# A channel product in seven products per pair of row tiles, and a reordered gate, in a three-part transformer kernel on one Trainium2 core

## The chip, the cores and the metric

The kernel runs on one core of a Trainium2 chip. The core has a matrix engine (TensorE, PE), which multiplies a stationary weight tile of 128 x 128 by a moving tile of up to 512 columns and adds into banks of PSUM; three engines for elementwise work (VectorE or DVE, ScalarE or ACT, GpSimd or POOL); and SyncE (SP), which here issues all DMA transfers. The engines run side by side, each in the order of its own instructions, and wait for each other through semaphores. The metric is the time of one execution in device microseconds. The time before is 1161.88 us, the median of 3 runs (1161.79 to 1162.14).

## The reference

Three parts on 8 batches of 576 tokens and 512 channels, each on the output of the one before: chunked attention, a mixer, a gated layer.

```
# 1 attention: 8 heads of 64, chunks of 64 tokens
scores = scale * q_c @ k_c.T;  attn = exp(scores - max) / (sum + 1e-9);  x = attn @ v_c
# 2 mixer: token product, then channel product
h  = relu(x.T @ w_tok1) @ w_tok2          # 576 -> 256 -> 576, over tokens
u  = x + h.T
h2 = relu(u @ w_ch1) @ w_ch2              # 512 -> 1536 -> 512, over channels
x  = u + h2
# 3 gated layer
h  = relu(x @ w_in);  u, v = split(h)     # 512 -> 1024, halves of 512
v_n = (v - mean(v)) / sqrt(var(v) + 1e-6)
v_s = w_spatial @ v_n + b_spatial         # 576 x 576, over tokens
out = (u * v_s) @ w_out                   # 512 -> 512
```

## The kernel before

All products are done in fp16 with both operands split: a high part (the value rounded to fp16) and a low part (the value less its high part). Each product is three products, high x high, high x low, low x high, added in PSUM in fp32. A split costs one copy for the high part, mostly on ACT, and one subtraction for the low part on DVE or POOL.

Per batch PE does, in this order: the first channel product (`ch1`, 12 row tiles m of 24 matmuls of 288 columns, inner dimension 4 x 128, weights `c1w` resident in SBUF); the second (`ch2`, four tiles of 72 matmuls of 288); two of the pending output projections of the batch before (`proj`, 12 matmuls of 512 columns each); the gate's v half (`gate_v`, five token tiles); the first token product of the *next* batch (`tok1`, 28 matmuls of 512); four gated blocks (`gated`: a `gate_u` of 24 matmuls and a `spatial` of 28, the u block ahead of the spatial block for m = 0 and behind it for the others); the second token product of the next batch (`tok2`, four tiles of 12 matmuls of 288); the remaining projections. Attention of later batches is cut in steps (`a_step`), which a clock puts in between: `pump` adds an estimate for each matmul and calls the steps that are due (`pumps`, `attention_from`, which spreads a batch's attention over a span of 118000 units of this clock).

PE's order is the order of the code (`manual_schedule`). The order on DVE, ACT, POOL and SP is made by a scheduler, which follows dependencies and priority (`high_priority`). Two pools matter here. PSUM's pool `pm` has four tiles of two banks each, used in turn; the matmuls of a new tile wait until the tile's last reader is done. The working pool `wrk` has three buffers under the tag "t", used in turn by the temporaries of normalization, residual and gate.

Line numbers of the kernel before that the prediction uses: L435 is the matmul in `products`; L458 and L462 the two loops of `tok1`, L465 and L466 its evictions (relu to the high part on ACT, low part on DVE); L473 to L475 the update of x behind `tok2` and its split; L482 the low part of the residual on POOL; L558 the eviction of a v block; L600 and L611 the reads of PSUM of spatial and u; L613 and L614 the split of the gated product; L221 and L267 attention's matmuls; L212, L256 and L286 elementwise work of attention; L143 the split of weights, in the lead-in.

## Time and profile before

| | |
|---|---|
| median of 3 runs | 1161.88 us (1161.79 to 1162.14) |
| profiled execution | 1162.57 us, span 1160.8 us |
| mean granted clock of TensorE | 0.994 |
| PE busy | 1130.3 us (97%), 11256 matmuls |
| DVE, ACT, POOL busy | 572.9, 356.2, 190.2 us (49%, 31%, 16%) |

The span runs from the first to the last instruction. A line of a timeline gives the start, the time from there to the modelled end, the engine, the program's line, the operation and tiles, and a count; in brackets stands the idle time before it and what ended it. Matmuls overlap, so the price of one is read from the distance of two starts. The granted clock is given as a share of 2.4 GHz: 0.50 is the lower level, 1.2 GHz.

### The profile page before, as it was taken

Reading aid. Unit: us, or ns where it says so; the run is one execution under the profiler, and the core shown is the slowest. Engines: PE = TensorE matmul, PEld = TensorE weight load, DVE = VectorE, ACT = ScalarE, POOL = GpSimd, SP = SyncE. Lnnn points to the kernel's source line nnn. Section 1 sums busy time; section 2 is a strip of 40 time slices with the busy share of each in tenths; the row PEclk is TensorE's granted clock in tenths of the full one; section 3 lists DMA queues with packets and bytes.
Section 4 is the critical chain, followed back from the end, with each engine's and each line's share of the span. In section 5 each row is a group of like instructions: output and inputs, shape, how many; then the busy total and the mean of one; then the engine's idle time right before and its main releaser. Section 6 shows DMA issues by size and latency. Waiting matters only on the chain. (4 is left out here: it accounts for less than half of the span.)

```text
span 1160.8 us, 25354 instructions
## 1 busy us (share of the span) xinstructions
PE 1130.3 (97%) x11256; PEld 810.2 (70%) x11256; DVE 572.9 (49%) x1020; ACT 356.2 (31%) x568; POOL 190.2 (16%) x185
## 2 busy tenths in 40 slices
PE   5898989999999999999999999999999999999998
PEld 5576747776667766777576775777666775777765
DVE  6999987443643236533454424653363322441141
ACT  3334443332333223332224313242233222221121
POOL 0000032111310123102221022211131021200020
PEclk9899999999999999999999999999999999999999
DMA  9357613333222222223123220232211011000001
GB/s 318 119 200 234 208 34 73 70 68 79 38 68 49 42 60 38 60 46 56 46 38 88 62 49 25 49 88 43 60 34 37 19 27 30 1 1 1 19 19 46
DMA packets 92157, 76.68 MB, mean 66 GB/s; under 512 B 67600, under 2 KB 76816, under 8 KB 89744
## 3 DMA queue, kind: packets, MB, share of 16 engines
q1 hardware_dynamic: 92048, 75.06, 25.3%
q8 instruction: 88, 1.44, 0.5%
q14 instruction: 21, 0.17, 0.1%
HBM read 51.45 MB, written 9.44 MB: 52 GB/s over the span
## 5 line engine op out<-in xcount | busy, mean ns | idle before, releaser
L435 PE MATMUL mp<-xb,c1w 128*128 128x288 f16 x2304 | 288.3, 286 | 4.4 <-DVE xb L475 2.5
L522 PE MATMUL mp<-hb,c2w 128*128 128x288 f16 x2304 | 288.8, 286 | 3.0 <-DVE c2w L143 2.9
L435 PEld LDWEIGHTS <-c1w 128*128 128x128 f16 x2304 | 223.5, 98 | 63.7 <-DVE c1w L143 3.0
L522 PEld LDWEIGHTS <-c2w 128*128 128x128 f16 x2304 | 223.0, 98 | 60.9 <-DVE c2w L143 4.6
L513 DVE SCALAR_TENSOR_TENSOR hb<-mp,hb 128x576 f16<-128x576 f32 x96 | 72.5, 755 | 146.6 <-ACT hb L512 146.6
L435 PE MATMUL mp<-spw,vn 128*128 128x288 f16 x896 | 115.8, 286 | 0.0
L512 ACT ACTIVATE hb<-mp 128x576 f16<-128x576 f32 x96 | 62.3, 649 | 148.0 <-PE mp L435 147.9
L435 PEld LDWEIGHTS <-vn 128*128 128x128 f16 x896 | 86.7, 98 | 22.0
L435 PE MATMUL mp<-xb,inw 128*128 128x288 f16 x768 | 99.3, 286 | 0.0
L627 PE MATMUL mp<-otw,gb 128*128 128x512 f16 x432 | 96.0, 379 | 0.0
L435 PEld LDWEIGHTS <-inw 128*128 128x128 f16 x768 | 75.1, 98 | 20.4
L548 PE MATMUL mp<-inw,xb 128*128 128x512 f16 x384 | 84.7, 379 | 0.4 <-DVE xb L482 0.4
L480 DVE SCALAR_TENSOR_TENSOR rt<-mp,xT 128x576 f32<-128x576 f32 x32 | 24.1, 755 | 106.8 <-PE mp L522 106.8
L627 PEld LDWEIGHTS <-gb 128*128 128x128 f16 x432 | 42.1, 98 | 48.0
L482 POOL TENSOR_TENSOR xb<-rt,xb 128x576 f16<-128x576 f32 x22 | 30.4, 1384 | 275.1 <-ACT xb L481 275.1
L548 PEld LDWEIGHTS <-xb 128*128 128x128 f16 x384 | 37.3, 98 | 45.4 <-DVE xb L482 0.9
L286 POOL TENSOR_TENSOR xh<-xT,xh 128x512 f16<-128x512 f32 x24 | 27.8, 1158 | 247.4 <-ACT xh L283 226.4
L249 POOL TENSOR_TENSOR p<-sd,p 128x512 f16<-128x512 f32 (+1 forms) x30 | 34.7, 1156 | 159.9 <-ACT p L246 144.8
L481 ACT ACTIVATE xb<-rt 128x576 f16<-128x576 f32 x32 | 21.7, 681 | 126.3 <-DVE rt L480 126.3
L564 DVE BATCH_NORM_STATS2 st<-vt 128x6 f32<-128x512 f32 (+1 forms) x40 | 27.5, 690 | 58.2 <-ACT vt L558 57.9
L613 ACT ACTIVATE gb<-gt 128x576 f16<-128x576 f32 x32 | 21.8, 683 | 108.0 <-DVE gt L611 107.9
L435 PE MATMUL mp<-t2w,hb 128*128 128x288 f16 x384 | 50.3, 286 | 0.3 <-ACT hb L465 0.3
(144 smaller groups left out, 1137.8 us busy)
## 6 DMA issues: line engine op xcount, KB each, us to landing
qk<-in_qk SPq DMA_DIRECT2D x96, 128.0 KB, 2.8
out<-o SPq DMA_DIRECT2D x31, 256.0 KB, 2.0
v<-in_v SPq DMA_DIRECT2D x56, 128.0 KB, 3.3
vn<-in_wc SPq DMA_DIRECT2D x4, 1024.0 KB, 4.9
otw<-in_wc SPq DMA_DIRECT2D x3, 1024.0 KB, 4.8
spw<-in_wc SPq DMA_DIRECT2D x3, 1024.0 KB, 4.9
hb<-in_qk SPq DMA_DIRECT2D x4, 512.0 KB, 6.1
qk<-in_qk SPq DMA_DIRECT2D x4, 512.0 KB, 5.0
```

The costliest lines, as they stand in the source:

```text
L249: POOL.tensor_tensor(out=p_hl[rows, 1], in0=m["sd"][rows], in1=p_hl[rows, 0], op=ALU.subtract)
L286: POOL.tensor_tensor(out=m["lo"], in0=xT[:, :, tk], in1=m["hi"], op=ALU.subtract)
L435: PE.matmul(out=o, lhsT=l, rhs=r, start=(i == 0), stop=(i == len(seq) - 1))
L480: DVE.scalar_tensor_tensor(out=t, in0=ps, scalar=DN10, in1=two(x[:, m]), op0=ALU.mult, op1=ALU.add)
L482: eng.tensor_tensor(out=xl, in0=t, in1=xh, op=ALU.subtract)
L512: ACT.activation(out=hh, in_=ps, func=AF.Relu)
L513: DVE.scalar_tensor_tensor(out=hlo, in0=ps, scalar=0.0, in1=hh, op0=ALU.max, op1=ALU.subtract)
L522: PE.matmul(out=o, lhsT=c2w[:, a, k, mc], rhs=hb[:, k, r, s], start=(k + e == 0), stop=(k == 11 and e == 2))
L548: PE.matmul(out=ps, lhsT=l, rhs=r, start=(k + e == 0), stop=(k == 3 and e == len(seq) - 1))
L564: DVE.bn_stats(out=st[0:n], in_=t[0:n])
L613: ACT.activation(out=gh, in_=t, func=AF.Copy)
L627: PE.matmul(out=ps, lhsT=gb[:, l, k, tk], rhs=otw[:, r, k], start=(k == 0 and e == 0), stop=(k == 3 and e == 2))
```

## The change

For batches 2 to 7 `ch1` is replaced by `ch1_fast`. The 1536 output channels are six pairs p of row tiles; the product of a pair, inner dimension 512, and of the 576 columns is seen as a 2 x 2 block product: a11 to a22 are blocks of the weights (128 channels by 256), b11 to b22 blocks of x (256 channels by 288 tokens). It is done with seven products instead of eight, Winograd's form of Strassen's method, each of six matmuls of 288 columns. The sums of x (q1, q2, q3 and q1 again, `first_sums`) are made and split behind `tok2`; the sums of the weights (`sum_steps`, 30 steps in batch 1) are split and written to DRAM (`c1s`) and streamed back (`stream`), 128 KB for each product, in 18 slots in the place of `c1w`. Results are joined in PSUM, where two products can be added in place, and by DVE (`u2b`, `vb`, `c22`, `c`); the four blocks of hb are its output, whose layout changes, so that `ch2` reads it block by block.

The gate: u blocks are computed by `gate` between the v blocks (in batches 0 and 7 behind them) and kept in SBUF as `uall`; `gated` is then the spatial block and a multiplication of two tiles in SBUF. `tok2` moves in front of the spatial blocks, directly behind `tok1`. All four or five pending projections go behind `ch2`. The low parts of the gate go to POOL for all m except for the last one of the last batch, and the carry copies from DVE to ACT and POOL. The clock of attention's steps is scaled by `PACE` per stage, over a span of 112000.

Line numbers of the changed kernel that the prediction uses: L627 is the matmul in `product`; L504 the low part in `split`; L509 the update of x in `first_sums`; L515, L519, L521 and L523 the sums q1, q2, q3 and q1 again; L645 the sum `u2b`; L754 the read of the spatial block from PSUM; L766 the multiplication by `uall`; L769 the low part of the gated product; L450 the matmul in `products`, L477 the second loop of `tok1`. L241 to L254 and L225, L269 (DVE), L262 and L299 (POOL) are attention.

```diff
-    hb = new("hb", [128, 12, 2, S])
+    hb = new("hb", [128, 6, 2, 4, 288])
...
+    SLOTS = 18
+    ORDER = [(p, n) for p in range(7) for n in ((p, 0), (p, 4), (p - 1, 6), (p - 1, 2), (p, 3), (p, 5), (p, 1)) if 0 <= n[0] < 6]
+    ORDER = [n for _, n in ORDER]
+    uall = hall[:, 4608:9216].bitcast(F32).rearrange("p (m t) -> p m t", m=4)
+    tq4 = new("tq4", [128, 2, 2, 288])
+    quad = lambda t: t.rearrange("p (e k t) -> p e k t", e=2, k=2)
+    tq = [xb[:, :, 0:2, 288:576], quad(call[:, 9216:10368]), quad(call[:, 10368:11520]), tq4]
+    vals = vall.bitcast(F32)
+    s1b, u2b, vb, c22b = vals[:, 0:288], [vals[:, 288 + 288 * i:576 + 288 * i] for i in range(2)], vals[:, 864:1152], [
+        vals[:, 1152 + 288 * i:1440 + 288 * i] for i in range(2)]
+    c1s = tc.dram_tile([6, 128, 3584], F16, name="c1s")
...
-        clock[0] += cols / 2.4 + 2.5
+        t = cols / 2.4 + 2.5
+        clock[0] += t
+        slow[0] += t * pace[0]
         for p in pumps:
-            while p[3]() and clock[0] >= p[0]:
+            while p[3]() and p[4][0] >= p[0]:
...
+    PACE = {"first": 0.5, "pair": 0.8, "ch1": 1.0, "ch2": 1.2, "gate": 1.0, "tok1": 1.0, "last": 0.6}
+    sums = {}
+
+    def split(t, hi, lo, eng=DVE):
+        ACT.activation(out=hi, in_=t, func=AF.Copy)
+        eng.tensor_tensor(out=lo, in0=t, in1=hi, op=ALU.subtract)
+
+    def first_sums(ps, m, x):
+        t1, t2 = slice(0, 288), slice(288, 576)
+        xm = two(x[:, m])
+        DVE.scalar_tensor_tensor(out=xm, in0=ps, scalar=DN10, in1=xm, op0=ALU.mult, op1=ALU.add)
+        s = t1 if m < 2 else slice(0, 576)
+        split(x[:, m, s], xb[:, 0, m, s], xb[:, 1, m, s])
+        b11, b12, b21, b22 = x[:, 0:2, t1], x[:, 0:2, t2], x[:, 2:4, t1], x[:, 2:4, t2]
+        if m == 1:
+            sums[0] = t = wrk.tile([128, 2, 288], F32, tag="t", name="q1")
+            DVE.tensor_tensor(out=t, in0=b12, in1=b11, op=ALU.subtract)
+            split(t, tq[0][:, 0], tq[0][:, 1], POOL)
+        if m == 3:
+            q1, q2, q3 = sums[0], wrk.tile([128, 2, 288], F32, tag="t", name="q2"), wrk.tile([128, 2, 288], F32, tag="t", name="q3")
+            DVE.tensor_tensor(out=q2, in0=b22, in1=q1, op=ALU.subtract)
+            split(q2, tq[1][:, 0], tq[1][:, 1], POOL)
+            DVE.tensor_tensor(out=q3, in0=b22, in1=b12, op=ALU.subtract)
+            split(q3, tq[2][:, 0], tq[2][:, 1], POOL)
+            DVE.tensor_tensor(out=q1, in0=b21, in1=q2, op=ALU.subtract)
+            split(q1, tq[3][:, 0], tq[3][:, 1], POOL)
...
+            if fast:
+                return first_sums(ps, m, x)
...
-        hh, hlo = two(hb[:, m, 0]), two(hb[:, m, 1])
+        row = slice(m % 2 * 2, m % 2 * 2 + 2)
+        hh, hlo = hb[:, m // 2, 0, row], hb[:, m // 2, 1, row]
...
+    def stream(upto):
+        while streamed[0] < min(upto, 42 * (B - FIRST_FAST)):
+            p, n = ORDER[streamed[0] % 42]
+            SP.dma_start(out=call[:, streamed[0] % SLOTS * 512:streamed[0] % SLOTS * 512 + 512],
+                         in_=c1s[p, :, 512 * n:512 * n + 512])
+            streamed[0] += 1
+
+    used = [0]
...
+        def first():
+            POOL.tensor_tensor(out=s[:, 0], in0=a21, in1=a22, op=ALU.add)
+            POOL.tensor_tensor(out=s[:, 2], in0=a11, in1=a21, op=ALU.subtract)
+
+        def second():
+            POOL.tensor_tensor(out=s[:, 1], in0=s[:, 0], in1=a11, op=ALU.subtract)
+            POOL.tensor_tensor(out=s[:, 3], in0=a12, in1=s[:, 1], op=ALU.subtract)
+
+        def high():
+            ACT.activation(out=g[:, :, 0], in_=s, func=AF.Copy)
+
+        def low():
+            DVE.tensor_tensor(out=g[:, :, 1], in0=s, in1=g[:, :, 0], op=ALU.subtract)
+            SP.dma_start(out=c1s[p, :, 1536:3584], in_=vall[:, 0:2048])
+
+        return [join, first, second, high, low]
...
+        def product(o, p, n, b, start):
+            assert ORDER[used[0] % 42] == (p, n)
+            i = used[0] % SLOTS * 512
+            w = call[:, i:i + 512].rearrange("p (e k m) -> p e k m", e=2, k=2)
+            o = o[:, 0:288]
+            for k in range(2):
+                for i, (a, e) in enumerate(((0, 0), (0, 1), (1, 0))):
+                    PE.matmul(out=o, lhsT=w[:, a, k], rhs=b[:, e, k], start=(start and k + i == 0),
+                              stop=(k == 1 and i == 2), skip_group_check=not start)
+                    pump(288)
+            used[0] += 1
+            stream(used[0] + SLOTS)
+
+        def relu2(c, hi, lo):
+            ACT.activation(out=c, in_=c, func=AF.Relu)
+            split(c, hi, lo, POOL)
+
+        for p in range(7):
+            pace[0] = PACE["first" if p < 1 else "pair"]
+            if p < 6:
+                ab[p] = a = pm.tile([128, 2, 512], F32, tag="m", name="mp")
+                product(a[:, 0], p, 0, xb[:, :, 0:2, t1], True)
+                product(a[:, 1], p, 4, tq[1], True)
+                with high():
+                    ACT.activation(out=s1b, in_=a[:, 0, 0:288], func=AF.Copy)
+                    DVE.tensor_tensor(out=u2b[p % 2], in0=a[:, 1, 0:288], in1=s1b, op=ALU.add)
+            if p:
+                d, u = cd[p - 1], u2b[(p - 1) % 2]
+                product(d[:, 0], p - 1, 6, xb[:, :, 2:4, t2], False)
+                product(d[:, 1], p - 1, 2, tq[3], False)
+                c = wrk.tile([128, 2, 288], F32, tag="t", name="c")
+                with high():
+                    DVE.tensor_tensor(out=c, in0=d[:, :, 0:288], in1=u.rearrange("p (a t) -> p a t", a=1).to_broadcast([128, 2, 288]), op=ALU.add)
+                    relu2(c, hb[:, p - 1, 0, 1:3], hb[:, p - 1, 1, 1:3])
+            if p < 6:
+                cd[p] = d = pm.tile([128, 2, 512], F32, tag="m", name="mp")
+                c22 = c22b[p % 2]
+                product(d[:, 0], p, 3, tq[0], True)
+                product(d[:, 1], p, 5, tq[2], True)
+                with high():
+                    DVE.tensor_tensor(out=vb, in0=d[:, 0, 0:288], in1=u2b[p % 2], op=ALU.add)
+                    DVE.tensor_tensor(out=c22, in0=d[:, 1, 0:288], in1=vb, op=ALU.add)
+                    relu2(c22, hb[:, p, 0, 3], hb[:, p, 1, 3])
+                product(a[:, 0], p, 1, xb[:, :, 2:4, t1], False)
+                with high():
+                    x1, hi, lo = a[:, 0, 0:288], hb[:, p, 0, 0], hb[:, p, 1, 0]
+                    ACT.activation(out=hi, in_=x1, func=AF.Relu)
+                    DVE.scalar_tensor_tensor(out=lo, in0=x1, scalar=0.0, in1=hi, op0=ALU.max, op1=ALU.subtract)
...
-            DVE.tensor_scalar(out=t[0:64], in0=t[0:64], scalar1=0.0, scalar2=2.0 ** -11, op0=ALU.max, op1=ALU.mult)
+            ACT.activation(out=t[0:64], in_=t[0:64], func=AF.Relu, scale=2.0 ** -11)
...
+    def gate(m):
+        ps = gate_u(m)
+        with tc.high_priority():
+            keep("a", ACT.activation(out=two(uall[:, m]), in_=ps, func=AF.Relu))
+
     def gated(m, b, eng):
-        if m == 0:
-            ps = gate_u(m)
         t = spatial(m)
-        if m:
-            ps = gate_u(m)
         with tc.high_priority():
-            DVE.scalar_tensor_tensor(out=t, in0=ps, scalar=0.0, in1=t, op0=ALU.max, op1=ALU.mult)
+            DVE.tensor_tensor(out=t, in0=t, in1=two(uall[:, m]), op=ALU.mult)
         gh, gl = two(gb[:, 0, m, 64:640]), two(gb[:, 1, m, 64:640])
         ACT.activation(out=gh, in_=t, func=AF.Copy)
         eng.tensor_tensor(out=gl, in0=t, in1=gh, op=ALU.subtract)
         if b % 2 == 0:
-            carry(m)
-
-    def carry(m):
-        for e in range(2):
-            DVE.tensor_copy(out=gb[:, e, m, 0:64], in_=gb[:, e, m, 576:640])
+            ACT.activation(out=gb[:, 0, m, 0:64], in_=gb[:, 0, m, 576:640], func=AF.Copy)
+            eng.tensor_copy(out=gb[:, 1, m, 0:64], in_=gb[:, 1, m, 576:640])
...
+            if b == FIRST_FAST - 1:
+                todo_sums = [f for p in range(6) for f in sum_steps(p)]
+                sum_pump = [clock[0], 2200.0, sum_next, lambda: len(todo_sums) > 0, clock]
+                pumps.append(sum_pump)
+            pace[0] = PACE["ch1"]
+            for m in range(12 if b < FIRST_FAST else 0):
                 if b == 0:
                     w_until(4 + m // 2)
                 ch1(m)
+            if b >= FIRST_FAST:
+                ch1_fast()
...
+                stream(SLOTS)
...
-            for i in pend[:2]:
+            for i in pend:
                 proj(b - 1, i)
...
+                if 0 < b < B - 1 and j < 4:
+                    gate(j)
+            if b == B - 1:
+                fin()
+            if b in (0, B - 1):
+                for m in range(4):
+                    gate(m)
             if b < B - 1:
                 a_until(b + 1)
                 pumps[:] = pumps[1:]
+                pace[0] = PACE["tok1"]
                 last = tok1()
-                attention_from(b + 2, 0.0, 118000.0)
+                attention_from(b + 2, 0.0, 112000.0)
                 with tc.issue_after(last):
                     fin()
-            else:
-                for i in pend[2:]:
-                    proj(b - 1, i)
-                fin()
+                pace[0] = PACE["last"]
+                for m in range(4):
+                    tok2(m, xTs[(b + 1) % 2], fast=b + 1 >= FIRST_FAST)
             for m in range(4):
-                gated(m, b, DVE if m == 3 else POOL)
+                gated(m, b, DVE if m == 3 and b == B - 1 else POOL)
...
-                for m in range(4):
-                    tok2(m, xTs[(b + 1) % 2])
                 w_until(len(W))
-                held = 4 if b == B - 2 else 2
                 pend = list(range(5 if b % 2 else 4))
-                for i in pend[:-held]:
-                    proj(b, i)
-                pend = pend[-held:]
```

On PE, behind the first token product made in batch 3 (`t1w` are its weights), with the semaphores that each instruction waits for. Before, the u block of the gate (`inw`) follows:

```order
L462 MATMUL mp<-x_93,t1w 128x512
L462 LDWEIGHTS t1w
L462 MATMUL mp<-x_93,t1w 128x512
L435 LDWEIGHTS inw
L435 MATMUL mp<-xb,inw 128x288 [waits Activation_49]
```

Now the second token product (`t2w`, with the evicted first one, `hb`, as weights) follows:

```order
L477 MATMUL mp<-x_93,t1w 128x512
L477 LDWEIGHTS t1w
L477 MATMUL mp<-x_93,t1w 128x512
L450 LDWEIGHTS hb [waits Activation_49]
L450 MATMUL mp<-t2w,hb 128x288 [waits PE_49]
```

The u block is gone from this place, and the first weights to be loaded are what ACT evicts from the product just ended.

On DVE, in the same place of a later batch, from the gated blocks on to the channel product. Before, the gated blocks (`gt`) end, each with one operand in PSUM (`mp`), and the second token product's update of x follows:

```order
L600 SCALAR_TENSOR_TENSOR gt<-mp,bB 128x576
L611 SCALAR_TENSOR_TENSOR gt<-mp,gt 128x576
L620 COPY gb<-gb 128x64 x2
L600 SCALAR_TENSOR_TENSOR gt<-mp,bB 128x576
L611 SCALAR_TENSOR_TENSOR gt<-mp,gt 128x576
L614 TENSOR_TENSOR gb<-gt,gb 128x576
L473 SCALAR_TENSOR_TENSOR xT_92<-mp,xT_92 128x576
```

Now the sums of x (q) and two blocks of attention stand ahead of the gated blocks and among them, and L645 of the first pair behind:

```order
L269 SCALAR_TENSOR_TENSOR v_88<-v_87,v_88 128x512
L519 TENSOR_TENSOR q_7771<-xT_91,q_7686 128x576
L504 TENSOR_TENSOR xb<-xT_91,xb 128x576
L521 TENSOR_TENSOR q_7772<-xT_91 128x576
L523 TENSOR_TENSOR q_7686<-xT_91,q_7771 128x576
L754 SCALAR_TENSOR_TENSOR gt<-mp,bB 128x576
L766 TENSOR_TENSOR gt<-gt,hb 128x576
L241 TENSOR_REDUCE mx<-mp 128x8
L225 TENSOR_TENSOR qk_86<-qk_85,qk_86 128x1024
```

The second operation of a gated block has both operands in SBUF now (`gt` and `hb`, where `uall` lies), and the order ends, thirteen instructions on, with the last gated block, L645, L660 and L661.

On POOL, the same stage. Before, low parts of the gated blocks (L614) and of attention alternate:

```order
L581 TENSOR_TENSOR vn<-vt,vn 128x512
L572 TENSOR_TENSOR y<-z,mhalf 64x1
L286 TENSOR_TENSOR xh<-xT_91,xh 128x512
L614 TENSOR_TENSOR gb<-gt,gb 128x576
L249 TENSOR_TENSOR p_89<-sd,p_89 128x512
L614 TENSOR_TENSOR gb<-gt,gb 128x576 x2
```

Now the low parts of the four sums stand ahead of four gated low parts (L769), and those of the pairs' results follow:

```order
L504 TENSOR_TENSOR xb<-q_7686,xb 128x2x288
L299 TENSOR_TENSOR xh<-xT_92,xh 128x512
L504 TENSOR_TENSOR c1w<-q_7771,c1w 128x576
L504 TENSOR_TENSOR c1w<-q_7772,c1w 128x576
L504 TENSOR_TENSOR tq_99<-q_7686,tq_99 128x576
L769 TENSOR_TENSOR gb<-gt,gb 128x576 x2
L262 TENSOR_TENSOR p_89<-sd,p_89 128x512
L769 TENSOR_TENSOR gb<-gt,gb 128x576 x2
L504 TENSOR_TENSOR hb<-vn,hb 128x288
```

POOL's row of this stage is eight instructions long up to the last gated low part.

## Rows read from the trace of the kernel before

**Rows 1.** The page, part 1: busy time, share of the span, instructions.
```profile
PE 1130.3 (97%) x11256; PEld 810.2 (70%) x11256; DVE 572.9 (49%) x1020; ACT 356.2 (31%) x568; POOL 190.2 (16%) x185
```
**Rows 2.** Waits on PE: line waited for: us in total, times, longest.
```profile
PE mp L267 <- DVE hb L466: 0.9, 4, 0.2
```
**Rows 3.** Timeline of PE, 300 to 350 us.
```profile
303.77 3.10 PE L435 MATMUL mp<-xb,inw 128*128 128x288 f16 x24
306.71 0.78 PE L435 MATMUL mp<-spw,vn 128*128 128x288 f16 x5
307.72 0.57 PE L267 MATMUL mp<-pT,v 64*64 64x64 f16 x48 [0.23 <-DVE hb L466]
...
337.88 7.93 PE L627 MATMUL mp<-otw,gb 128*128 128x512 f16 x36
345.65 4.57 PE L435 MATMUL mp<-xb,c1w 128*128 128x288 f16 x36
```
**Rows 4.** Timeline of PE, 150 to 176 us.
```profile
154.81 2.75 PE L458 MATMUL mp<-x,t1w 128*128 128x512 f16 x12
...
159.73 4.39 PE L458 MATMUL mp<-x,t1w 128*128 128x512 f16 x12 [2.17 <-ACT vt L558]
163.96 1.03 PE L462 MATMUL mp<-x,t1w 128*128 128x512 f16 x4
...
167.76 1.88 PE L435 MATMUL mp<-spw,vn 128*128 128x288 f16 x14
170.97 0.57 PE L221 MATMUL mp<-qk 64*64 64x64 f16 x48 [1.33 <-DVE hb L466]
```
**Rows 5.** Windows: us; busy PE, PEld, DVE, ACT, POOL (instructions); clock; DMA; GB/s.
```profile
160.00:162.00 2.00, 2.00 (x6) 0.76 (x5) 1.61 (x3) 0.56 (x1) 1.41 (x2) 0.50 0.52 152
50.00:54.00 4.00, 1.91 (x15) 1.44 (x15) 3.91 (x6) 1.06 (x2) 0.00 (x0) 1.00 0.00 0
```
**Rows 6.** Timeline of PE, 38 to 56 us.
```profile
40.14 1.03 PE L462 MATMUL mp<-x,t1w 128*128 128x512 f16 x4
41.42 6.29 PE L435 MATMUL mp<-t2w,hb 128*128 128x288 f16 x48 [0.26 <-ACT hb L465]
47.55 1.14 PE L435 MATMUL mp<-xb,c1w 128*128 128x288 f16 x8
52.09 4.19 PE L435 MATMUL mp<-xb,c1w 128*128 128x288 f16 x32 [2.30 <-DVE xb L475]
```
**Rows 7.** Groups by line: count, busy us, mean ns, idle before and releaser.
```profile
L475 DVE TENSOR_TENSOR xb<-xT,xb 128x576 f16<-128x576 f32 x32 | 24.1, 755 | 7.2 <-ACT xb L474 7.0
L474 ACT ACTIVATE xb<-xT 128x576 f16<-128x576 f32 x32 | 21.8, 683 | 28.4 <-DVE xT L473 27.9
L212 DVE TENSOR_TENSOR qk<-qk,qk 128x1024 f16<-128x1024 f32 (+1 forms) x30 | 33.2, 1108 | 0.0
L256 DVE SCALAR_TENSOR_TENSOR v<-v,v 128x512 f16<-128x512 f32 (+1 forms) x30 | 19.1, 636 | 33.2 <-ACT v L253 33.1
```
**Rows 8.** The instructions of L482: duration ns, shortest, median, longest; first and last start.
```profile
L482 POOL TENSOR_TENSOR xb<-rt,xb x22: 1274/1276/2074, 134.1 to 1088.2; 128x576 f16<-128x576 f32 x22
```
**Rows 9.** Timelines of DVE and POOL, two stretches of later batches.
```profile
412.49 1.22 DVE L212 TENSOR_TENSOR qk<-qk,qk 128x1024 f16<-128x1024 f32 x1
412.77 2.07 POOL L482 TENSOR_TENSOR xb<-rt,xb 128x576 f16<-128x576 f32 x1 [3.34 <-ACT xb L481]
...
863.42 0.76 DVE L611 SCALAR_TENSOR_TENSOR gt<-mp,gt 128x576 f32<-128x576 f32 x1
862.78 1.16 POOL L286 TENSOR_TENSOR xh<-xT,xh 128x512 f16<-128x512 f32 x1 [5.05 <-PE mp L435]
```
**Rows 10.** Timeline of SP's queue, 330 to 350 us.
```profile
333.28 1.25 SPq L250 DMA_TRANSPOSE pT<-p  x1
...
343.26 0.53 SPq L639 DMA_DIRECT2D out<-o  x1
```
**Rows 11.** The page, part 6: DMA issues, KB each, median us to landing.
```profile
qk<-in_qk SPq DMA_DIRECT2D x96, 128.0 KB, 2.8
```

More of the change, by code (lines that the diff above doesn't have):

```diff
@@ L468, in tok1, with keep, behind @@
         return last
+    FIRST_FAST = 2
+    tail = {}
+    def keep(name, op):
+        tail[name] = op.ins
+        return op
+    def behind():
+        stack = ExitStack()
+        for ins in tail.values():
+            stack.enter_context(tc.issue_after(ins))
+        return stack
+    PACE = {"first": 0.5, "pair": 0.8, "ch1": 1.0, "ch2": 1.2, "gate": 1.0, "tok1": 1.0, "last": 0.6}
[22 more added lines that the diff above has]
+            split(q1, tq[3][:, 0], tq[3][:, 1], POOL)
     def first_residual(ps, m, x):
@@ L479, in residual, with tok2 @@
         t = wrk.tile([128, 2, 288], F32, tag="t", name="rt")
-        DVE.scalar_tensor_tensor(out=t, in0=ps, scalar=DN10, in1=two(x[:, m]), op0=ALU.mult, op1=ALU.add)
-        ACT.activation(out=xh, in_=t, func=AF.Copy)
+        keep("d", DVE.scalar_tensor_tensor(out=t, in0=ps, scalar=DN10, in1=two(x[:, m]), op0=ALU.mult, op1=ALU.add))
+        keep("a", ACT.activation(out=xh, in_=t, func=AF.Copy))
         eng.tensor_tensor(out=xl, in0=t, in1=xh, op=ALU.subtract)
-    def tok2(m, x, split=False):
+    def tok2(m, x, split=False, fast=False):
         outs, ps = psum2()
@@ new lines, in mixer_kernel, with sum_steps, join @@
+    streamed = [0]
+    def stream(upto):
[5 more added lines that the diff above has]
+    used = [0]
+    def sum_steps(p):
+        f = vals[:, 0:1024].rearrange("p (k m) -> p k m", k=4)
+        s = vals[:, 1024:2048].rearrange("p (n k m) -> p n k m", n=4, k=2)
+        g = vall[:, 0:2048].rearrange("p (n e k m) -> p n e k m", n=4, e=2, k=2)
+        a11, a12, a21, a22 = f[:, 0:2, 0:128], f[:, 2:4, 0:128], f[:, 0:2, 128:256], f[:, 2:4, 128:256]
+        w = c1w[:, :, p]
+        o = c1s[p].rearrange("p (n e k m) -> p n e k m", n=7, e=2, k=2)
+        def join():
+            DVE.tensor_tensor(out=f, in0=w[:, 0], in1=w[:, 1], op=ALU.add)
+            for n, (k, c) in enumerate(((0, 0), (2, 0), (2, 128))):
+                for e in range(2):
+                    SP.dma_start(out=o[:, n, e], in_=w[:, e, k:k + 2, c:c + 128])
+        def first():
[10 more added lines that the diff above has]
+        return [join, first, second, high, low]
@@ L520, in ch2 @@
                 for e, (a, r) in enumerate(((0, 0), (0, 1), (1, 0))):
-                    for o, s in zip(pss[i][0], HALF):
-                        PE.matmul(out=o, lhsT=c2w[:, a, k, mc], rhs=hb[:, k, r, s], start=(k + e == 0), stop=(k == 11 and e == 2))
+                    for t, o in enumerate(pss[i][0]):
+                        PE.matmul(out=o, lhsT=c2w[:, a, k, mc], rhs=hb[:, k // 2, r, k % 2 * 2 + t], start=(k + e == 0), stop=(k == 11 and e == 2))
                         pump(288)
@@ L557, in gate_v @@
         if j < 4:
-            ACT.activation(out=t, in_=ps, func=AF.Relu, scale=2.0 ** -11)
+            keep("a", ACT.activation(out=t, in_=ps, func=AF.Relu, scale=2.0 ** -11))
         else:
@@ L684, in attention_from @@
                 end = a_end(b)
-                pumps.append([clock[0] + skip, span / (end - todo[0]), a_step, lambda: todo[0] < end])
+                pumps.append([slow[0] + skip, span / (end - todo[0]), a_step, lambda: todo[0] < end, slow])
         def held_tick():
@@ L697, in mixer_kernel, with sum_next @@
                 pumps[0][1] = 1700.0
-            for m in range(12):
+            def sum_next():
+                with behind():
+                    todo_sums.pop(0)()
+            if b == FIRST_FAST - 1:
[4 more added lines that the diff above has]
+            for m in range(12 if b < FIRST_FAST else 0):
                 if b == 0:
@@ L708, in mixer_kernel @@
                 last = ch2(ms, x)
+            if b == FIRST_FAST - 1:
+                while todo_sums:
+                    todo_sums.pop(0)()
+                pumps.remove(sum_pump)
+                stream(SLOTS)
             if b == 0:
@@ L720, in mixer_kernel @@
                     gate_v_part(ps, j, ks)
+            pace[0] = PACE["gate"]
             for j in range(5):
```

23 lines of the change are left out of this document (15 added, 8 removed).

## The prediction, made before the changed kernel ran

> **What bounds the kernel now.** I read the engine totals first. TensorE (PE) is busy 1130.3 us of a span of 1160.8, while VectorE (DVE), ScalarE (ACT) and GpSimd (POOL) are at half or less [rows 1]. PE's work stands in a hand-written order, so the time is that work plus the waits in it. I looked at PE's waits next: those of the steady batches are tiny, one of 0.9 us in total for the four attention blocks behind the first token product [rows 2]. The rest lies in the first batch. So the question is how many matmuls go, which waits in PE's order go, and which come. PE's timeline gives the price of a matmul: 24 of 288 columns issue from 303.77 to 306.71, or 0.1225 us each, and 36 of 512 columns from 337.88 to 345.65, or 0.2158 us each [rows 3].
>
> The profiled execution took 1162.57 us; the median of the runs is 1161.88. I make the sum against 1162.57 and take off 0.69 at the end.
>
> **a. Fewer products.** A batch's first channel product has 288 matmuls of 288 columns before. After, batches 2 to 7 do six pairs of row tiles with seven products of six matmuls: 252. That is 36 x 6 = 216 matmuls less, at 0.1225 us: **-26.46 us**. All lie on PE, which is the path.
>
> **b. The waits of the first batch.** In batch 0 PE idles behind the gate's v blocks. Twelve matmuls of 0.2158 us from 154.81 end at 157.40, the next starts at 159.73: 2.33 us. After that idle the granted clock is 0.50 (1.2 GHz) [rows 5]; the next 12 take until 163.96, 4.23 us for 2.59, so 1.64 more. Fourteen of 288 from 167.76 end at 169.48, the next starts at 170.97: 1.50 us [rows 4]. After the change four u blocks of 2.94 us, and then the second token product, stand at these places and cover both waits: 2.33 + 1.64 + 1.50, **-5.47 us**.
>
> **c. The attention block behind the first token product.** In the steady batches it waits for the PSUM tile that DVE frees: five matmuls from 306.71 end at 307.32, the block starts at 307.72, 0.40 us, in four batches [rows 2, 3]. It now comes later: **-1.60 us**.
>
> **d. The second token product right behind the first.** Before, some 25 us of gated work stood between them, except in the first batch's lead, where PE shows what the direct succession costs. Four matmuls of 0.2158 from 40.14 end at 41.00, the next starts at 41.42: 0.42. Forty-eight of 0.1225 then end at 47.30, the next starts at 47.55: 0.25 [rows 6]. The order now has this succession in seven batches, with eviction and split of the first product in front of it: 0.67 x 7 = **+4.69 us**.
>
> **e. Inside the seven products.** Each pair reuses two PSUM tiles that DVE frees by two additions, and DVE also carries attention. One product is 6 x 0.1225 = 0.735 us, about the eviction that has to be done beside it (a DVE addition of 576 columns takes 0.755 [rows 7], of 288 about 0.45, an estimate). From the order I expect 0.3 us per batch at the last pair, where nothing follows to hide it: **+1.80 us**.
>
> **f. From the spatial stage into the products.** Here I expect the most. Count from the end of the first token product. The second token product is 4 x 12 matmuls with 0.67 of waits and one attention block (0.51): it ends at 7.06. Four spatial products of 28 matmuls (3.43 each), with one attention block, end at 21.29. Four products of the first pair take 2.94, so the fifth, which the order makes wait for DVE's L645, is due at 24.23. L645 stands on DVE behind all four gated blocks. With nothing else in the way it ends at 21.29 + 2 x 0.755 + 0.45 + 0.2 of hand-overs = 23.45, in time. Of DVE's work behind the second token product the residual and one low part are done by about 9.0 (7.06 + 2 x 0.755 + hand-overs). From there to L645 DVE has eight instructions with two operands in SBUF of 0.755 (L519, L504, L521, L523 and four L766), two of attention at 0.64 and one of 1.108: 8.43 us [rows 7]. POOL has five low parts of 576 columns at 1.276 [rows 8] and two of attention at 1.16 [rows 9]: 8.70 us. The trace shows such a pair excluding each other: POOL's L482 began while DVE's L212 ran, and took 2.07 us where 1.276 is usual. With one operand in PSUM, DVE's L611 and POOL's L286 overlap at their usual 0.76 and 1.16 [rows 9]. If all of it goes in turn, L645 ends at 9.0 + 8.43 + 8.70 + 0.45 + 0.2 = 26.8, 2.57 us late. The gated temporaries have only three buffers, shared with the sums, so the spatial products wait for the same chain, and the idle shows there or at L645. That holds for the products of batches 2 to 5; batch 6 has one attention instruction fewer before it (2.0), batch 7 has none: 4.7 us less, in time. 4 x 2.57 + 2.0 = **+12.3 us**. After idles of about this size the clock fell in one place (2.33 us, 1.64 lost, above) and stayed in two (2.30 before 52.09 [rows 6], with the clock at 1.00 around it [rows 5]; 1.33 before 170.97 [rows 4]); I take two of five: **+3.3 us**.
>
> This cost is not in the trace of before, so it has two ends. Below, 0: POOL's and DVE's turns fall where the other is idle or reads PSUM. Above: one more POOL turn (1.276) and one ACT copy (0.683) [rows 7] are waited for as well, 4.5 us, with a fall of the clock each time: 5 x (4.5 + 1.64) = 30.7. I take the middle, since the count of turns comes from the order and the price of each from rows.
>
> The Trainium skill, page "SBUF — State Buffer", section "Who interferes with whom", states the general form: a DVE instruction with two SBUF inputs and a GpSimd instruction that reads SBUF hold a shared port in turn, whichever issued first blocking the other for its whole length, while one SBUF input does not contend. The rows above agree, 2.07 against 1.276 us and no loss with PSUM. By this rule every pair of the stage excludes, which gives the sum here; without it the sum would lack the 15.6 us of f. It is the rule that speaks against the change.
>
> **Parts at nothing.** The sums of weights in batch 1 (30 steps) run on idle POOL, ACT and DVE under 288 second channel products and first ones of 70 us; if that cover went, it would cost one batch a few us. Carry copies go to ACT and POOL, both idle there. The projections keep their count, only their place. The u blocks' evictions (ACT, 0.683 [rows 7]) lie under 2.6 to 2.9 us of matmuls each. SP issues 42 loads per batch, at 0.53 us as the row of an output has it, 22.3 us, with two transposes of 1.25 and six other loads among them (5.7 us) [rows 10]: 28 us in a window of 252 x 0.1225 + 1.3 = 32 us, and 18 slots (13.2 us) of lead.
>
> **Sum.** 1162.57 - 26.46 - 5.47 - 1.60 + 4.69 + 1.80 + 12.3 + 3.3 = 1151.1; less 0.69, **1150.4 us**.
>
> **Rivals.**
> A. Turns do not collide. Then f is 0: 1150.4 - 15.6 = **1134.8** (1133 to 1139, with e and d at half or double). For it: L645 needs only 23.45 without collisions, and DVE, with 49% busy, has room. Against it: 17 us of excluding work stand in 15 us.
> B. The stream of weights is late, and the kernel becomes slower than before. Each load stands in SP's queue among the attention's transposes; where a load costs SP 1.25 us like a transpose [rows 10], a batch needs 42 x 1.25 + 5.7 = 58.2 us, 13 more than window and lead: 13 x 6 = 78, **about 1228**. It decides above (32 + 13.2 - 5.7) / 42 = 0.94 us per load, and makes the kernel slower than before above 0.99. Against it: the plain loads' 0.53, and landing times of 2.8 us for 128 KB [rows 11].
> C. The stalls of f at their upper end, each with the clock at 1.2 GHz for a stretch: 1150.4 - 15.6 + 30.7 = **1165.5** (1159 to 1166), no gain. For it: the spatial products may wait as well as the fifth product. Against it: it asks for five falls, where two of three idles shown kept the clock.
>
> **Chances.** Forecast 0.53 (its own range 1141 to 1159), A 0.27, C 0.13, B 0.07. About 0.2% (2.3 us) is what a measurement of this kernel can tell from no change: 1159.5 to 1164.2 is the same. Of C some half lies there, little of the forecast: faster 0.84, same 0.07, slower 0.09. The range takes A's lower part in and most of C: 1134 to 1163.
>
> **What would show it.** Right: PE with 216 matmuls less; in the profile of after, PE's idle before the products' line (L627) of 2 to 3 us at the first pair, released by DVE or POOL, five times; POOL rows of 576 columns of 2 us where 1.276 is usual; no wait of L458's kind in batch 0. A shows as L627 without waits and PE near 99% busy. B shows as waits of L627 for the DMA of c1s. C shows as a granted clock near 0.5 behind each spatial stage. The forecast is wrong if the idles lie elsewhere, above all in the first token product to second (d) or within the pairs (e), which I priced from one place of the trace.

## The result and the profile after

The changed kernel takes 1150.99 us (median of 4 runs, 1149.55 to 1153.72) against 1162.01 us for the kernel before in the same runs: a ratio of 0.9908, 95% interval 0.9887 to 0.9929. Its profiled execution took 1149.73 us, with a span of 1147.9 us; the forecast's sum for it was 1151.1.

The engine totals show what went and what came (busy time, share of the span, instructions):

```profile
PE 1106.4 (96%) x11040; PEld 787.2 (69%) x11040; DVE 651.1 (57%) x1117; ACT 458.6 (40%) x798; POOL 344.6 (30%) x328
```

There are 216 matmuls less than in [rows 1], and POOL has nearly twice the work. The waits on PE from 140 to 1140 us (us in total, times, longest) are the steps of the forecast:

```profile
PE mp L627 <- DVE vn L645: 9.0, 5, 2.1
PE mp L627 <- DVE vn L661: 2.3, 6, 0.4
PE mp L450 <- ACT hb L480: 1.8, 7, 0.3
PE mp L450 <- ACT vt L712: 0.4, 1, 0.4
PE mp L450 <- DVE vt L715: 0.2, 1, 0.2
```

L645 is waited for five times (step f), L661 once per batch at the last pair (e), L480 behind each of the seven first token products (d). The waits behind v blocks (L712, L715) are 0.4 and 0.2 us, where [rows 4] has 2.17; the second wait there, 1.33, is not in the list (b). PE's timeline around one transition:

```profile
312.02 1.03 PE L477 MATMUL mp<-x,t1w 128*128 128x512 f16 x4
313.31 6.05 PE L450 MATMUL mp<-t2w,hb 128*128 128x288 f16 x46 [0.26 <-ACT hb L480]
...
336.58 0.90 PE L627 MATMUL mp<-c1w 128*128 128x288 f16 x6
339.35 1.63 PE L627 MATMUL mp<-xb,c1w 128*128 128x288 f16 x12 [1.86 <-DVE vn L645]
```

The product that starts at 336.58 needs 6 x 0.1225, to 337.32; the fifth product starts at 339.35, 2.03 us later. (The bracket counts from a modelled end, 0.17 after that.) DVE and POOL in the same stage:

```profile
321.79 0.68 DVE L269 SCALAR_TENSOR_TENSOR v<-v,v 128x512 f16<-128x512 f32 x1
322.39 1.71 DVE L519 TENSOR_TENSOR q<-xT,q 128x576 f32<-128x576 f32 x1
324.02 0.75 DVE L504 TENSOR_TENSOR xb<-xT,xb 128x576 f16<-128x576 f32 x1
...
325.35 1.83 DVE L523 TENSOR_TENSOR q<-xT,q 128x576 f32<-128x576 f32 x1
...
329.47 1.69 DVE L225 TENSOR_TENSOR qk<-qk,qk 128x1024 f16<-128x1024 f32 x1
...
336.14 1.15 DVE L766 TENSOR_TENSOR gt<-gt,hb 128x576 f32<-128x576 f32 x1
...
338.00 0.93 DVE L766 TENSOR_TENSOR gt<-gt,hb 128x576 f32<-128x576 f32 x1
338.85 0.45 DVE L645 TENSOR_TENSOR vn<-mp,vn 128x288 f32<-128x288 f32 x1
```

```profile
321.88 1.60 POOL L299 TENSOR_TENSOR xh<-xT,xh 128x512 f16<-128x512 f32 x1 [1.30 <-issue]
324.89 3.44 POOL L504 TENSOR_TENSOR c1w<-q,c1w 128x576 f16<-128x576 f32 x2 [1.41 <-ACT c1w L503]
328.29 1.79 POOL L504 TENSOR_TENSOR tq<-q,tq 128x576 f16<-128x576 f32 x1
...
335.40 1.28 POOL L769 TENSOR_TENSOR gb<-gt,gb 128x576 f16<-128x576 f32 x1 [3.10 <-ACT gb L768]
```

L519 takes 1.71 us and L523 1.83, where the same operation takes 0.75 in L504 at 324.02; L225 takes 1.69, where 1.22 is its own time (the experiment without the low parts shows it; the 1.108 of [rows 7] is a mean over two forms). Each began while a row of POOL ran. L769 at 335.40 keeps its usual 1.28 beside a read of PSUM (L754, 335.36), and holds L766 at 336.14, which takes 1.15. Over the stage DVE loses 0.96 + 1.08 + 0.47 and, at the L766, 0.7: 3.2 us. L645 ends at 339.30; 3.2 us earlier is 336.1, and the forecast's end without collisions (23.45 after 312.88) is 336.3, both before 337.32.

### The profile page after: what moved, and what is told of

It is laid out like the page before. It is cut to its first block, busy times and chain, and to the rows that moved or that the text cites. A ratio compares the mean times of both kernels' runs of the same rounds, so it can differ in the third digit from the quotient of the medians.

```text
span 1147.9 us, 26048 instructions
## 1 busy us (share of the span) xinstructions
PE 1106.4 (96%) x11040; PEld 787.2 (69%) x11040; DVE 651.1 (57%) x1117; ACT 458.6 (40%) x798; POOL 344.6 (30%) x328
## 4 chain that ended last, share of the span: by engine, by line
PE 74%; DVE 18%; issue 3%; ACT 2%; DMA 2%; POOL 1%; SPq 0%; DVEq 0%; ACTq 0%; POOLq 0%
PE mp L676 22%; PE mp L450 16%; PE mp L627 14%; PE mp L779 8%; PE mp L702 7%; PE mp L473 4%; DVE gb L147 2%; DVE gb L143 2%; DVE gt L754 1%; PE mp L234 1%; DVE xT L509 1%; PE mp L280 1%; DVE gb L141 1%; DVE gt L766 1%; DVE qk L225 1%
## 5 line engine op out<-in xcount | busy, mean ns | idle before, releaser
L676 PE MATMUL mp<-hb,c2w 128*128 128x288 f16 x2304 | 289.6, 286 | 4.5 <-DVE c2w L156 4.4
L676 PEld LDWEIGHTS <-c2w 128*128 128x128 f16 x2304 | 222.6, 98 | 62.2 <-DVE c2w L156 5.7
L627 PEld LDWEIGHTS <-c1w 128*128 128x128 f16 x1512 | 147.2, 98 | 50.3 <-issue 13.3
L627 PE MATMUL mp<-xb,c1w 128*128 128x288 f16 x864 | 125.1, 286 | 11.2 <-DVE vn L645 9.0
L450 PE MATMUL mp<-spw,vn 128*128 128x288 f16 x896 | 112.3, 286 | 0.0
L450 PEld LDWEIGHTS <-vn 128*128 128x128 f16 x896 | 87.1, 98 | 22.0
L450 PE MATMUL mp<-xb,inw 128*128 128x288 f16 x768 | 99.4, 286 | 0.6 <-ACT vt L712 0.4
L450 PEld LDWEIGHTS <-inw 128*128 128x128 f16 x768 | 74.8, 98 | 24.7 <-issue 1.0
L702 PE MATMUL mp<-inw,xb 128*128 128x512 f16 x384 | 88.2, 379 | 0.5 <-ACT xb L536 0.3
L450 PE MATMUL mp<-xb,c1w 128*128 128x288 f16 x576 | 73.8, 286 | 4.4 <-DVE xb L530 2.5
L504 POOL TENSOR_TENSOR hb<-c,hb 128x576 f16<-128x576 f32 x36 | 46.1, 1281 | 95.4 <-ACT hb L503 95.4
L450 PEld LDWEIGHTS <-c1w 128*128 128x128 f16 x576 | 55.3, 98 | 19.9 <-DVE c1w L156 3.0
L262 POOL TENSOR_TENSOR p<-sd,p 128x512 f16<-128x512 f32 (+1 forms) x30 | 36.8, 1226 | 97.2 <-ACT p L259 85.8
L627 PE MATMUL mp<-c1w 128*128 128x288 f16 x432 | 64.7, 286 | 0.0
L769 POOL TENSOR_TENSOR gb<-gt,gb 128x576 f16<-128x576 f32 x31 | 48.4, 1566 | 47.0 <-ACT gb L768 47.0
```

Of the source, the lines that this page charges most:

```text
L262: POOL.tensor_tensor(out=p_hl[rows, 1], in0=m["sd"][rows], in1=p_hl[rows, 0], op=ALU.subtract)
L450: PE.matmul(out=o, lhsT=l, rhs=r, start=(i == 0), stop=(i == len(seq) - 1))
L504: eng.tensor_tensor(out=lo, in0=t, in1=hi, op=ALU.subtract)
L627: PE.matmul(out=o, lhsT=w[:, a, k], rhs=b[:, e, k], start=(start and k + i == 0), stop=(k == 1 and i == 2), skip_group_check=not start)
L676: PE.matmul(out=o, lhsT=c2w[:, a, k, mc], rhs=hb[:, k // 2, r, k % 2 * 2 + t], start=(k + e == 0), stop=(k == 11 and e == 2))
L702: PE.matmul(out=ps, lhsT=l, rhs=r, start=(k + e == 0), stop=(k == 3 and e == len(seq) - 1))
```

## Experiments

Theory 1 is the forecast's account: DVE's and POOL's turns on two-operand work in SBUF add up in full. Rivals and a second theory are named where they come in. Ratios are to the kernel before. Spans of single profiles differ by some microseconds in the lead-in (the first token product ends between 39 and 43 us), so the waits in the traces decide.

**The reorder alone.**

```diff
-    FIRST_FAST = 2
+    FIRST_FAST = 8        # no batch with seven products, no sums
```

> The gate's new order, the second token product ahead of the spatial blocks and all other parts stay, but all batches keep the first channel product with 288 matmuls. Theory: the reorder alone is worth little; the waits of batch 0 and of the attention block go (-5.2 + 0.9 and -1.2 us as the trace of the changed kernel has them), and the direct succession of the token products comes (7 x 0.65 = +4.5): about 1161 us. The sums of x are gone from the stage, so no stall ahead of the first channel product. Rival: the multiplication of two tiles in SBUF and POOL's low parts make the stall by themselves; then ten us more, about 1171.

Measured: 1163.93 us, ratio 1.0007 (0.9997 to 1.0016). The trace has the seven waits for L480 and no wait ahead of the first channel product. The reorder by itself gains nothing that can be told (1161 was expected), and makes no stall; the rival falls.

**The seven products alone.**

```diff
-                if 0 < b < B - 1 and j < 4:
-                    gate(j)
...
+            DVE.scalar_tensor_tensor(out=t, in0=ps, scalar=0.0, in1=t, op0=ALU.max, op1=ALU.mult)   # gated, ps = gate_u(m)
...
+                for m in range(4):      # behind the gated blocks, proj behind it
+                    tok2(m, xTs[(b + 1) % 2], fast=b + 1 >= FIRST_FAST)
```

> The seven products in batches 2 to 7 stay; the gate, the spatial blocks, the second token product and the projections stand in the order of the kernel before, with the u block read from PSUM. Theory (DVE and POOL taking turns in the spatial stage make the stall): the sums of x now lie beside two or three projections (5.2 to 7.8 us) and need about 3.6 us to the first split, so they are covered except in the last transition, which has no projection (about 4 us): 1162 - 26.5 + 3.5 (waits inside the products) + 4 = about 1143 us, less than with the reorder. Rival: the sums need the spatial stage as cover; without it about 4 us stand open in each of six transitions, 1163 us.

Measured: 1176.44 us, ratio 1.011 (1.0094 to 1.0127), slower than before, far from my 1143 and above the rival's 1163 too. Waits on PE, a sum of x on DVE, and a stretch behind one of the waits (columns as in [rows 5]):

```profile
PE mp L627 <- DVE vn L645: 12.1, 4, 3.8
PE mp L234 <- DVE hb L481: 4.3, 1, 4.3
PE mp L627 <- DVE vn L661: 3.8, 8, 0.9
PE mp L627 <- POOL c1w L504: 3.6, 3, 1.5
PE mp L627 <- ACT c1w L503: 2.4, 1, 2.4
```

```profile
489.17 1.83 DVE L523 TENSOR_TENSOR q<-xT,q 128x576 f32<-128x576 f32 x1
```

```profile
496.00:500.00 4.00, 3.55 (x15) 2.16 (x15) 1.77 (x4) 1.18 (x3) 1.46 (x2) 0.50 0.67 206
```

The projections did not cover the sums: PE waits for their splits (L503, L504) themselves, and the splits on POOL block DVE there as well, L523 for 1.83 us as in the changed kernel. Behind the idle before 496.45 the clock is at 0.50, 1.2 GHz. The 4.3 us for L481 lie in batch 0 and are none of the sums' doing. So the reorder, worth nothing alone, is what makes the seven products pay. That the spatial blocks are the cover is argued: the reorder moves the gate, the second token product and the projections together, and they were not taken apart.

**The sums' low parts on DVE.**

```diff
-            split(q2, tq[1][:, 0], tq[1][:, 1], POOL)     # q3 and q1 alike
+            split(q2, tq[1][:, 0], tq[1][:, 1], DVE)
```

> The low parts of the last three sums of x are made on DVE (0.755 us each) and not on POOL (1.276 each). Theory: the two engines take turns, so the sum of both counts: 3 x (1.276 - 0.755) = 1.56 us less per transition; the five waits for L645 fall from 2.0 to 2.2 us to about 0.6, and the time to about 1143 us. Rival: DVE's own queue is what is late, and it gets 3 x 0.755 = 2.3 us longer: waits of about 4.3 us, about 1161 us.

Measured: 1148.91 us, ratio 0.9881 (0.9866 to 0.9896). The waits for L645:

```profile
PE mp L627 <- DVE vn L645: 7.8, 5, 1.8
```

Four of 1.93 us by the distance of starts, neither 0.6 nor 4.3: nearly as before. In this stage DVE ran without a gap to speak of (322.89 to 341.33 us in the first transition), L523 took 0.75 us and L225 1.21; three instructions more took the place of the time it had been blocked. From this came theory 2: DVE's queue sets the end of L645, and POOL counts only as far as it blocks an instruction of DVE.

**More work on POOL, reading or only writing.**

```diff
+                for _ in range(2):
+                    POOL.tensor_tensor(out=scr[:, 0:576], in0=bB, in1=bB, op=ALU.add)
+                    # the other kernel: POOL.memset(scr, 0.0)
```

> POOL gets two more instructions per transition, of 576 columns, whose operands lie in SBUF (it adds a constant to itself; nobody reads the result), one on either side of the low part of q1. Theory 1, the prediction's sum (both engines' turns count in full): 2 x 1.276 = 2.55 us more per transition, the waits for L645 go from 2.0 to 2.2 us to about 4.7, the time to about 1163 us. Theory 2, formed from the run with the sums on DVE (DVE is busy or blocked without a gap, and only what it is blocked counts): one or two more of DVE's instructions meet a POOL instruction and lose about 1 us each, waits of 3 to 4 us, about 1157 us. Rival (POOL's reads don't hold DVE up): waits as before, 1150 us.

> The same two places on POOL hold a fill of 1152 columns each, which reads nothing from SBUF and keeps POOL's queue busy in the same way. Theories 1 and 2: a fill does not hold DVE up, the waits for L645 stay near 2.0 to 2.2 us (up to 1 more where DVE waits for a buffer that POOL frees later), 1150 to 1153 us. Rival (the length of POOL's queue is the cause, not what it reads): the same rise as with the reads.

Measured: 1158.63 us, ratio 0.9972 (0.9950 to 0.9995) with reads, 1160.56, ratio 0.9972 (0.9960 to 0.9984) with fills. The waits, a row of POOL, one of DVE and a window behind the wait, with reads:

```profile
PE mp L631 <- DVE vn L649: 11.6, 5, 2.6
```

```profile
331.04 2.26 POOL L505 TENSOR_TENSOR tq<-q,tq 128x576 f16<-128x576 f32 x1
334.72 0.94 DVE L253 TENSOR_SCALAR mx<-mx 128x8 f32<-128x8 f32 x1
```

```profile
341.00:344.00 3.00, 2.94 (x13) 1.87 (x13) 1.38 (x4) 1.54 (x4) 2.02 (x3) 0.52 0.11 22
```

The waits, three rows of POOL and one of DVE, with fills:

```profile
PE mp L631 <- DVE vn L649: 11.8, 5, 2.5
```

```profile
330.49 1.06 POOL L526 MEMSET scr<- 128x1152 f32 x1
331.51 1.28 POOL L505 TENSOR_TENSOR tq<-q,tq 128x576 f16<-128x576 f32 x1
332.73 1.06 POOL L526 MEMSET scr<- 128x1152 f32 x1
```

```profile
331.69 2.17 DVE L226 TENSOR_TENSOR qk<-qk,qk 128x1024 f16<-128x1024 f32 x1
```

(L649 is L645 here, L505 L504, L226 L225, L253 L252.) With reads four of the waits rose by 0.6 us and the fifth by 0.3, not by 2.55: theory 1 is refuted, and theory 2 had its size too large. DVE's rows give the rise of the first: L253, of 0.16 us in the changed kernel, is held to 0.94, and L226 loses 0.13 us less than there. With fills I expected nearly no rise, and four waits rose by 0.5 us and the fifth by 1.0, as the rival said, which blamed the length of POOL's queue. The rows show a read at work all the same. L226 began 0.18 us after POOL's read of 331.51 and ended 1.07 us after that read's end at 332.79, near its own time of 1.22, with the second fill running beside it (332.73 to 333.79). A fill did not hold it; the first fill pushed the read onto it. So the sizes of the pair do not separate reads from fills: it matters which of DVE's instructions a POOL read meets.

Most of the 8 to 10 us lost against the changed kernel are clock. The waits rose by 2.7 and 2.9 us in all. Behind three of the five waits with reads, and four with fills, the granted clock was between 0.50 and 0.64. From the first wait for L649 to the one at the last pair PE took 29.90 us with reads, and from the third, behind which the clock stayed, 28.22: a fall cost 1.7 us here. Against the same stretches of the changed kernel all seven cost 1.6 to 1.7, 4.9 us with reads and 6.5 with fills.

**The low parts left out.** DVE's order is unchanged.

```diff
-            split(q2, tq[1][:, 0], tq[1][:, 1], POOL)     # q3 and q1 alike
+            ACT.activation(out=tq[1][:, 0], in_=q2, func=AF.Copy)
```

> The low parts of the last three sums of x are left out (POOL's three subtractions; the buffers keep what they hold), so the output is not the reference's; DVE's order is the same instruction by instruction. Theory 2 (DVE has no gap in the stage, and what it is blocked by POOL makes the lateness): in the changed kernel DVE loses 1.08 at L523, 0.58 at L225 and 0.1 at the first L766 to these three, so the waits for L645 fall by about 1.6 to 1.8, from 2.03 to 2.23 us to about 0.4, and batch 6's 1.25 goes: about 1142 us. Theory 1 (turns in full): 3.8 us less, no wait at all, 1140 us. Rival (DVE's own work alone is too long for the stage): waits stay at 2 us, 1150 us.

Measured: 1143.27 us (2 runs), ratio 0.9824 (0.9806 to 0.9842).

The waits on PE, and two rows of DVE in one transition:

```profile
PE mp L627 <- DVE vn L645: 1.3, 4, 0.4
```

```profile
326.56 0.75 DVE L523 TENSOR_TENSOR q<-xT,q 128x576 f32<-128x576 f32 x1
...
329.51 1.22 DVE L225 TENSOR_TENSOR qk<-qk,qk 128x1024 f16<-128x1024 f32 x1
```

L523 is back at 0.75 and L225 at 1.22. Four waits of 0.4 to 0.6 us are left by the distance of starts, and batch 6's is gone. Each of the four fell by 1.6 us, and DVE had lost 1.08 (L523), 0.47 (L225) and 0.09 (the first L766) to these reads, 1.64 in all: theory 2 in place and size. DVE's work alone is not too long, and POOL's turns don't count in full (no wait would be left).

**No attention in the stage.**

```diff
-    PACE = {... "last": 0.6}          attention_from(b + 2, 0.0, 112000.0)
+    PACE = {... "last": 0.0}          attention_from(b + 2, 0.0, 99000.0)
```

> The clock of attention's steps stands still from the first token product to the end of the spatial blocks (pace 0, with the span cut from 112000 to 99000 so that a batch's steps still end in time). Theory: attention's 2.4 us on DVE and 2.3 us on POOL leave the stage, as in the last transition, where nothing waits: the waits for L645 go to 0 and the time falls by 9.8 us to about 1141 us, as far as the denser attention costs nothing elsewhere. Rival: the three buffers of the temporaries are the cause, with or without attention: waits of 1.5 to 2 us stay, about 1150 us.

Measured: 1141.54 us, ratio 0.9816 (0.9801 to 0.9831). The waits for L645 are gone; those for L661 and L480 stay as they were, here the first:

```profile
PE mp L627 <- DVE vn L661: 2.3, 6, 0.4
```

The three buffers are not the cause by themselves.

**Cover by PE's order.** Three edits, one kernel each.

```diff
+    ORDER.remove((0, 1))                                # first: the fifth product later
+    ORDER.insert(ORDER.index((1, 4)) + 1, (0, 1))       # first_block(0) behind pair 1's two
...
+            if between and k == 0:                      # second, in ch2: products 6 and 2 of p = 5
+                between()
...
+                for i in pend[-1:]:                     # third, behind tok1
+                    proj(b - 1, i)
```

> The fifth product of the first pair is moved behind the first two products of the second pair, so that 12 matmuls (1.47 us) lie ahead of it; the stream's order follows. If L645 is late by itself, the waits fall by 1.47 to about 0.6, and batch 6's of 1.25 goes: -7.3 us, about 1143 us. Rival: the second pair's products need PSUM tiles that the same DVE chain frees (the tile of the third spatial block by L754), so the wait only moves ahead to them: about 1150 us.

> The last two products of the last pair are put behind the first six matmuls of the second channel product, in each of six batches. If the 0.54 us wait there is only DVE's addition (c22) that nothing covers, 0.735 us of matmuls cover it: -3.2 us against the changed kernel. Rival: the second channel product needs a PSUM tile that the same addition frees, so the wait moves: no change.

> One pending projection (12 matmuls of 512 columns, 2.59 us) moves from behind the second channel product to between the two token products, in the six transitions that have one; its place covers the two waits of 0.42 and 0.23 us there: 6 x 0.65 = -3.9 us in the trace. The wait for L645 is not touched by it in theory, since the stage starts with the second token product; but the scheduler puts attention's instructions elsewhere, which may move it by half a microsecond either way: 1147 us, 1144 to 1150. Rival: the projection's PSUM tile or its copy on ACT puts off the evictions of the token product, and the waits stay: 1150 us.

Measured, in this order: 1147.88 us, ratio 0.9867 (0.9847 to 0.9886); 1148.53, 0.9879 (0.9857 to 0.9902); 1150.04, 0.9879 (0.9865 to 0.9894). Waits on PE in the first of them:

```profile
PE mp L629 <- DVE vn L673: 2.8, 8, 0.7
PE mp L629 <- DVE vn L655: 2.0, 4, 0.6
```

With the later fifth product (L655 is L645, L673 is L661) the waits for it fell as expected, but waits for the addition behind it (L673) rose, 0.7 us for 0.4: DVE is late, and the next pair meets it. So the time lies between the two expected, 1143 and 1150. In the second kernel the wait at the last pair is gone from the list, as expected. In the third the waits of the token products went in the six transitions, and one of 2.35 us for L661 came in one batch, with a fall of the clock to 0.50. There L269 of attention stood ahead on DVE and was held by a low part on POOL (L269 took 1.35 us from 910.06, POOL's L504 ran from 909.58 to 910.85). The waits from 140 to 1140 us make 15.1 us in its trace, for 14.6 in the changed kernel, so the trace shows no gain of the 3.9 expected. The medians differ by 1 us, and the two ratios' intervals overlap.

**Together.** No attention in the stage, the last products in the second channel product, the projection between; then also no attention during the first pair.

```diff
-    PACE = {"first": 0.5, ...}        # the second kernel
+    PACE = {"first": 0.0, ...}
```

> Three edits at once: no steps of attention from the first token product to the end of the spatial blocks (which took the waits for L645 to 0 by itself, 1141.5 us), the last pair's last products behind the first matmuls of the second channel product (-3.2), and a projection between the token products (-3.9). If the three waits are separate, 1141.5 - 3.2 - 3.9 = about 1134.4 us, the fastest here. Rival: a projection in front of the second token product lets DVE start it later or the PSUM tiles run in another turn, and a part comes back: 1137 us or more.

> As the kernel before it (no attention in the spatial stage, last products behind matmuls of the second channel product, a projection between the token products), with attention held back during the first pair's products too (pace 0, span 96000). In that kernel the waits for the first pair's addition came back at 1.3 us, because an attention instruction (L269) stood on DVE ahead of it and was blocked by POOL. If that is the whole cause, the four waits of 1.31 and one of 1.04 go: 1139.1 - 6.3 = about 1132.8 us. Rival: the attention pushed out of the first pair crowds the later pairs, whose waits for the last addition return (2.5 us at one place in the kernel with the projection alone): 1136 to 1139 us.

Measured: 1139.09 us (5 runs, 1138.01 to 1140.29), ratio 0.9789 (0.9776 to 0.9802), the lowest median here, though not the sum expected (1134.4); the second 1140.14, ratio 0.9801 (0.9787 to 0.9814), not apart from it. In the first, waits for the first pair's addition (L654) came back, 1.31 us in four transitions. DVE there:

```profile
335.14 1.35 DVE L269 SCALAR_TENSOR_TENSOR v<-v,v 128x512 f16<-128x512 f32 x1 [1.27 <-ACT v L266]
336.41 0.45 DVE L654 TENSOR_TENSOR vn<-mp,vn 128x288 f32<-128x288 f32 x1
```

An instruction of attention, L269, waits for ACT at the head of DVE's queue and is then blocked, 1.35 us for 0.6, by POOL's low part that began at 334.67. In the second kernel it is gone from there, and the waits return in the later pairs (its rival); its longest wait on PE:

```profile
PE mp L627 <- DVE vn L664: 3.3, 5, 0.8
```

## Why the prediction was right

By its steps, each in the profiled execution; a wait is its bracket and 0.17 us.

| step | forecast | trace |
|---|---|---|
| a, 216 matmuls | -26.46 | -26.46 |
| b, batch 0 | -5.47 | -4.6: two waits of 0.5 and 0.4 us behind v blocks stay |
| c, attention block | -1.60 | -1.2: the blocks start 0.09 us late now, for 0.40 (29 matmuls from 320.05 end at 323.60, the block starts at 323.69) |
| d, token products | +4.69 | +4.5 (7 x 0.65) |
| e, last pair | +1.80 | +3.2 (6 x 0.54) |
| f, stall for L645 | +12.3 | +9.8 (2.03, 2.23, 2.04, 2.23, 1.25) |
| f, clock | +3.3 | 0 |

The column of the trace makes -14.8; the profiled executions differ by 12.84. Some 1.5 us of the rest is a longer wait for weights in the lead-in (L676 waits 4.4 us for them, L522 2.9 before). That the forecast, 1150.4 us, came within 0.6 us of the median is in part luck: f with its clock was 5.8 us too dear, b, c and e were 2.7 us too favourable, e most of all (0.54 us a batch for 0.3), and the lead-in was not in the sum.

**Step f** was right in place, releaser, number and nearly in size: L645 ends 26.4 us after the first token product (312.88 to 339.30), for 26.8. Its account of the size was wrong, and that the size came out was luck. It added POOL's 8.70 us in full, of which 3.2 show as longer instructions of DVE. And it left out DVE's reads of PSUM, which stand in its own queue (four L754 of 0.75, L241 and L242 of 0.68: 4.4 us). The two errors nearly cancelled. POOL's row was also miscounted ahead of the forecast: up to the last gated low part it has ten instructions, not eight. The cause, two engines excluding each other, is shown by the low parts left out: DVE's order is the same, L523 and L225 are at their own times, and the waits fall by the time by which they had been longer, 1.6 us. The rule of the Trainium skill, "SBUF — State Buffer", "Who interferes with whom", held in every pair shown here, the fill that only writes included (L226 ended beside it, 1.07 us after the read). The forecast had it that one SBUF input does not contend; that page of the Trainium skill says so only outside DVE's 2-port modes. L253, with one SBUF input, was held (0.94 us for 0.16); in which mode it ran no run shows.

**The clock** did not fall in the profiled execution. It fell behind the same wait in the kernel with the last products moved, and it may be part of the spread of the runs (1149.55 to 1153.72), of which the slowest has a mean clock of 0.991 for 0.995; but the one of 1152.25 us has 0.995, and neither was profiled, so this stays open.

**Rivals.** A fails, since the waits exist. Its time, 1134.8 us, needed the collisions gone; 1143.3 us were had with three POOL reads of each transition left out, and 1141.5 with attention out of the stage. B fails: no wait for the stream is in the list. C fails for this kernel, whose clock stayed; two POOL instructions more per transition come near it (1158.6 and 1160.6 us).

## What to carry to other kernels

Where a change gives VectorE and GpSimd two-operand work in SBUF in the same stage, list VectorE's queue in its order, add what each instruction loses to the GpSimd read that it meets, and compare its end with the time at which TensorE needs the result; adding both engines' work was no measure here. Other work that is free to move (here attention) should stay out of that stage. An edit that gains nothing alone can be what another needs, so both halves are worth a run.
